# The state product of a chunked linear-attention kernel, head by head into halves of the PSUM partitions

## The chip, the cores and the metric

The kernel runs on one core of a Trainium2 chip. The metric is device time in microseconds (us) from a run of the whole kernel; lower is better. The core has five engines with instruction queues of their own: TensorE (PE in the profile, with its weight loads as PEld), VectorE (DVE), ScalarE (ACT), GpSimd (POOL) and SyncE (SP, which here only issues transfers).

## The reference

Two stages, one after the other. The first is a recurrent attention with decay, for 4 batches x 8 heads x 768 steps, head size 48:

```python
for t in range(S):
    cur = np.einsum('bhd,bhe->bhde', u[None] * kt, vt)
    y[:, :, t] = np.einsum('bhd,bhde->bhe', rt, state + cur)
    state = wt[:, :, :, None] * state + np.einsum('bhd,bhe->bhde', kt, vt)
```

The second adds to each of the 3072 rows (384 wide) a mixture of adapters: 8 experts of rank 16, of which a gate picks two.

```python
logits = x @ w_gate                      # top 2 of 8, softmax over the two
delta[mask] += w[mask, k, None] * ((x[mask] @ A[e]) @ B[e])
return x + delta
```

## The kernel before

The 3072 rows are 24 tiles of 128 steps, six tiles (chunks) for each batch, and a tile holds all 8 heads side by side (8 x 48 = 384). Within a chunk the recurrence is turned into products: sums of the logarithms of the decay (`csA`, `csB`), their exponentials (`expP`, `expN`), decayed r and k (`mult`, line 284, on VectorE into `rk2`), transposes (`tr`, `trev`), scores of each head with a mask (`amm`, line 353, and `aev`, line 359), and y as scores times v (`ymA`, line 397) plus r times the state of the chunk before (`ymS`, line 387). The term with u goes through `rkp` (line 293), `dg` and `dv` (line 322). The second stage then works on the finished y (`xs`) by groups of up to four tiles: transposes (`xk`), gate (`lg`, `g1` to `g4`), and the two adapter products (`z`, `d`).

The state is what the change is about. In `rk2` each head has 64 columns, 48 of data and 16 of zeros, and heads stand in pairs p, with g = 0 or 1 for the first or second of a pair: 4 pairs, 128 columns each. The accumulator `S_acc` is 128 PSUM partitions x 384 f32, seen as (g, p, e). `kv` (line 366) multiplies, for each pair, the 128 columns of k of both heads with the 96 columns of v of both heads, over the 128 steps of the tile, four matmuls in all. Of the result for a pair the blocks k of head 0 with v of head 0 (first 64 partitions, g = 0) and head 1 with head 1 (last 64, g = 1) are wanted; the two crossed blocks are not. `sev` (through the helper's lines 303 on ScalarE or 305 on VectorE) copies the whole accumulator into `S_sb` as bf16, `szero` (line 382) writes zeros over the two crossed blocks, on GpSimd or, with ch = 1, on VectorE, and `ymS` of the next tile uses `S_sb` for both heads of a pair at once. The products with k of several tiles of a batch add up in `S_acc`; it is begun anew at the first chunk of each batch. The last chunk of a batch needs no `kv`, so there are 20 groups of `kv`, `sev` and `szero`.

The order of the work is written out by hand in `PLAN`, a list of words such as `kv:7` (function, tile) or `sev:3.1` (with ch = 1). Every engine carries out its own instructions in the order in which the list issues them, and waits by semaphore for what it reads. Loads of r, k and v from tile 2 on are issued on GpSimd's queue, those of w and the stores on SyncE's.

Two neighbours matter when the matmuls are compared. `amm` takes its operands from 48 partitions that begin at partition 0 or 64, so it uses a part of the rows of the array, while all other matmuls here use 128 rows and 128 columns. `ymA` is eight matmuls of 48 columns, each with weights of its own.

Of the kernel before, what the change touches and what calls it, by code (L numbers as in the profile page):

```python
# [36 lines left out]
aev:3 load_rk:16 xs:1.1 csA:6 trev:4 xk:1 szero:2 expP:6 load_w:8 ba:2.1 amm:4 xs:2.1 mult:5 dv:3 lg:0 szero:3.1
csB:6 tr:5 aev:4 load_w:10 xk:2 expN:6 csA:7 trev:5.1 ymS:3 load_v:16 xkev:1 xkev:2 ymS:4 dg:5 expP:7 ln:8 ymA:3
mult:6 ba:3 dg:4 csB:7 expN:7 load_w:12 rkp:6 amm:5 tr:6 xs:3 xk:3 dgev:5.1 kv:4 lg:2 dv:4 load_w:14 csA:8 trev:6
aev:5 ymA:4 ba:4 sev:4.1 amm:6 expP:8 lg:1 rkp:7 xs:4 szero:4 xkev:3 dv:5.1 csB:8 kv:6 mult:7 lg:3 g1:3 xk:4 expN:8  # L40
ymS:5 csA:9 dg:6 rkp:8 ln:12 xkev:4.1 tr:7 aev:6 load_w:16 expP:9 gexp:3 dg:7 load_B:0 ymA:5 trev:7 z:3 g2:3 ba:5.1
csB:9 dgev:7.1 sev:6 mult:8 expN:9 load_w:18 xs:5.1 amm:7 kv:7 g3:3 lg:4 csA:10 tr:8 ymA:6 sev:7 expP:10 trev:8 kv:8
xk:5 dv:6 aev:7 rkp:9 ba:6 csB:10 g4:3.1 mult:9 tr:9 sev:8 szero:7 kv:9 zw:3 zTm:3 dv:7.1 expN:10 xs:6 zTev:3 csA:11
szero:6 xkev:5 xk:6 trev:9 expP:11 amm:8 ymS:7 xkev:6 mult:10 szero:8 ba:7.1 csB:11 ymA:7 expN:11 dg:9 dg:8 rkp:10
tr:10 aev:8 sev:9.1 xs:7.1 castB:0 csA:12 expP:12 amm:9 ymS:8 dgev:9.1 mult:11 trev:10 xk:7 dv:8 aev:9 rkp:11 csB:12
ymA:8 expN:12 load_w:20 lg:6 tr:11 szero:9 ba:8 d:3.2 xkev:7 trev:11 xs:8 csA:13 lg:7 expP:13 lg:5 oev:3.2 g1:7 d:1
xk:8 csB:13 oev:1 xkev:8.1 expN:13 dv:9 amm:10 d:2 mult:12 ymS:9 csA:14 ba:9 kv:10 dg:10 gexp:7 ymS:10 g2:7 ln:16
ymA:9 aev:10 rkp:13.1 dg:11 dgev:11 tr:12 expP:14 sev:10 oev:2 rkp:12 xs:9 amm:11 dv:10.1 ymA:10 csB:14 aev:11
trev:12.1 expN:14 lg:8 kv:12 mult:13 ba:10.1 rkp:14.1 xs:10.1 g3:7 xk:9 csA:15 d:0.2 szero:10 xk:10 xkev:9 dg:12
expP:15 xkev:10 mult:14 dv:11.1 amm:12 oev:0.2 g4:7 sev:12 szero:12 csB:15 tr:13 expN:15 ymS:11 kv:13 dg:13 ba:11.1  # L50
trev:13 ymA:11 sev:13 csA:16 z:7 xs:11.1 expP:16 tr:14 dgev:13 mult:15 aev:12 zw:7 xk:11 load_w:22 store:0 csB:16
amm:13 lg:10 zTm:7 ymA:12 dv:12 xkev:11.1 ln:20 ba:12 kv:14 lg:11 expN:16 lg:9 trev:14 csA:17 aev:13 dv:13.1 rkp:15
g1:11 ymS:13 zTev:7.1 xs:12 ba:13.1 mult:16 expP:17 sev:14 tr:15 ymA:13 amm:14 xs:13.1 csB:17 gexp:11 xk:12 rkp:16
d:5 szero:13 g2:11 expN:17 xkev:12 xk:13 rkp:18 trev:15 csA:18 trd:16 dg:15 aev:14 expP:18 g3:11 g4:11 dg:14 mult:17
oev:5 z:11 amm:15 csB:18 store:3 dgev:15 kv:15 xkev:13 szero:14 ymS:14 dv:14 rkp:17.1 d:6 expN:18 ymA:14 dv:15 zw:11
csA:19 ba:14 aev:15 sev:15 oev:6 lg:12 ymS:15 szero:15 dg:16 kv:16 lg:13 ymA:15 expP:19 csB:19 ba:15 xs:14 expN:19
amm:16 rkp:19 xk:14 mult:18 zTm:11 sev:16 xs:15 csA:20 kv:18 d:4 xkev:14 aev:16 rkp:21 trd:17 zTev:11.1 xk:15 dg:17
store:1 amm:17 expP:20 ymS:16 oev:4 mult:19 dgev:17 sev:18 ymA:16 csB:20 kv:19 d:8.2 store:2 rkp:22.1 dv:16.1
xkev:15 trd:18 dv:17.1 lg:14 d:11 aev:17 expN:20 ba:16.1 sev:19 csA:21 oev:8.2 mult:20 trd:19 amm:18 xs:16.1 expP:21
lg:15 xk:16 d:9.2 dg:18 csB:21 oev:11 aev:18 szero:16 oev:9.2 ymS:17 rkp:20 ba:17.1 store:5 ymA:17 xkev:16 trd:20  # L60
expN:21 dg:19 kv:20 xs:17.1 amm:19 store:6 csA:22 xk:17 sev:20 szero:19 szero:18 dgev:19 dv:18 mult:21 expP:22 lg:16
# [1 line left out]
xk:18 trd:21 gexp:15 xk:19 sev:21 csA:23 oev:7 dg:20 xkev:18 xkev:19 store:9 expP:23 szero:20 rkp:23 ymS:20 lg:17
aev:20 g2:15 dg:21 lg:18 lg:19 store:7 mult:22 dgev:21 store:11 dv:20.1 amm:21 csB:23 kv:22 z:15 store:10 store:4
ymA:20 ba:20.1 tr:22 g3:15 ymS:21 expN:23 g4:15 aev:21 xs:20.1 ymA:21 zw:15 dv:21 mult:23 ba:21 xk:20 trev:22 zTm:15
xkev:20 amm:22 zTev:15.1 g1:19 tr:23 gexp:19 g2:19 xs:21 sev:22 xk:21 aev:22 d:15 dg:23 store:8 dg:22 d:13.2
# [25 lines left out]
def kernel(  # L92
# [49 lines left out]
    def setD(t, ch):  # L142
        nc.vector.memset(ones, 1.0)
        nc.vector.memset(centre, CENTRE / 128)

    def triangle(o, cmp, base, step):
        nc.gpsimd.affine_select(out=o, in_=ones[:, 0:128], compare_op=cmp, fill=0.0, base=base,
                                pattern=[[step, 128]], channel_multiplier=-step)
# [212 lines left out]
        st[t]["at"] = at  # L361

    def kv(t, ch):
        c = t % NC
        for p in range(P):
            nc.tensor.matmul(S_acc[:, :, p, :],  # L366
                             lhsT=st[t]["rk2"][:, 1, p].rearrange("s a b -> s (a b)"),
                             rhs=st[t]["v16"][:, 2 * p:2 * p + 2, :],
                             start=(c == 0 and p == 0), stop=(p == P - 1), skip_group_check=True)
# [9 lines left out]

    def szero(t, ch):  # L380
        for g in range(2):
            (nc.gpsimd, nc.vector)[ch].memset(st[t]["S"][64 - 64 * g:128 - 64 * g, g], 0.0)  # L382
# [215 lines left out]
```

## Time and profile before

| | us |
|---|---|
| median of 2 runs (85.8 to 85.84) | 85.82 |
| profiled execution, its own time | 85.61 |
| span of its trace | 83.9 |
| TensorE busy | 76.5 (91%), 1214 matmuls |
| VectorE busy | 72.1 (86%), 166 instructions |
| ScalarE busy | 68.3 (81%), 163 instructions |
| GpSimd busy | 57.1 (68%), 113 instructions |

The span runs from the first to the last instruction of the trace; the profiled execution's time is 1.7 us longer than it. A line of a group gives line, engine, operation, what is written and read, shapes and count; then busy time, and mean ns of one. A line of the timeline gives start, duration until the last of the group ends, engine, line and count; a bracket at the end is idle time of the engine just before, and what ended it. Records of matmuls overlap, since each goes in long before the one ahead of it has come out, so start to start is the measure of what one costs.

### The profile page before, as it was taken

What the parts mean: (1) busy time and instruction counts of PE and PEld (TensorE: products, weight loads), DVE (VectorE), ACT (ScalarE), POOL (GpSimd) and SP (SyncE); (2) the same over time, 40 slices, a digit from 0 to 9 for tenths busy, and PEclk for the clock granted to TensorE, in tenths of its full rate; (3) what the DMA queues carried; (4) which work ended last, traced back from release to release, by engine and by line L of the source; (5) the groups of instructions that cost most, each with busy time, mean ns of one, the idle gap of its engine ahead of it and who ended that gap; (6) DMA issues with size and microseconds to landing.
All of it is one profiled execution on the core that took longest, in us unless ns stands there. A gap on an engine that the chain in (4) does not pass through costs nothing.

```text
span 83.9 us, 3133 instructions
## 1 busy us (share of the span) xinstructions
PE 76.5 (91%) x1214; PEld 56.8 (68%) x1214; DVE 72.1 (86%) x166; ACT 68.3 (81%) x163; POOL 57.1 (68%) x113
## 2 busy tenths in 40 slices
PE   3979999999989999999999999999999999998730
PEld 1234568866868879786888887788677898775300
DVE  3007979997999999999999999999999999999650
ACT  1564988999997999899999989979999949878400
POOL 4987925979949798687864697896969581832000
PEclk9999999999999999999999999999999999999995
DMA  0999999999999999999999992997889672272763
GB/s 13 328 388 283 272 289 281 275 272 293 282 211 214 262 254 252 287 293 283 226 212 212 208 225 55 221 295 140 125 200 225 204 289 90 99 281 109 277 250 129
DMA packets 15407, 19.10 MB, mean 228 GB/s; under 512 B 7200, under 2 KB 12320, under 8 KB 15392
## 3 DMA queue, kind: packets, MB, share of 16 engines
q1 hardware_dynamic: 11952, 11.63, 43.5%
q0 software_dynamic: 3152, 6.69, 41.7%
q10 hardware_dynamic: 288, 0.59, 2.1%
q8 instruction: 9, 0.15, 0.7%
q14 instruction: 6, 0.05, 0.2%
HBM read 19.29 MB, written 4.72 MB: 286 GB/s over the span
## 4 chain that ended last, share of the span: by engine, by line
PE 76%; DVE 6%; ACT 6%; DMA 4%; issue 2%; DVEq 1%; ACTq 0%
PE xk_ps L421 10%; PE trp L332 8%; PE a_ps L353 8%; PE y_ps L397 5%; PE cs_ps L254 5%; PE z_ps L497 4%; PE d_ps L534 4%; PE cs_ps L250 4%; PE a_ps L173 4%; DMA w<-in_w_dram 4%; PE s_ps L366 4%; PE y_ps L387 4%; PE cs_ps L245 4%; PE d_ps L533 3%; PE y_ps L403 2%
## 5 line engine op out<-in xcount | busy, mean ns | idle before, releaser
L359 DVE TENSOR_TENSOR at<-a_ps,strict 128x1024 f16<-128x1024 f32 x24 | 29.3, 1220 | 1.2 <-PE a_ps L353 0.8
L322 POOL TENSOR_TENSOR dv<-v,dg 128x384 f16<-128x384 f16 (+1 forms) x24 | 20.4, 859 | 8.6 <-ACT dg L303 4.7
L293 POOL TENSOR_TENSOR rkp<-rk 128x384 f16<-128x384 f16 (+1 forms) x16 | 14.6, 916 | 0.8 <-DMA rk<-in_rk_dram 0.7
L263 ACT ACTIVATE e<-cs_ps 128x384 bf16<-128x384 f32 x24 | 11.9, 494 | 3.3 <-PE cs_ps L254 3.0
L259 ACT ACTIVATE e<-cs_ps 128x384 bf16<-128x384 f32 x24 | 12.1, 503 | 1.6 <-PE cs_ps L250 1.4
L284 DVE TENSOR_TENSOR rk<-rk,e 128x768 bf16<-128x768 f16 x22 | 12.8, 582 | 0.0
L332 PE MATMUL trp<-ident,rk 128*128 128x128 bf16 x144 | 11.1, 219 | 0.4 <-DVE rk L284 0.4
L309 ACT COPY xkT<-xk_ps 128x384 f32<-128x384 f32 (+1 forms) x24 | 10.5, 447 | 0.9 <-PE xk_ps L421 0.6
L382 POOL MEMSET S_sb<- 64x192 bf16 x38 | 9.6, 252 | 2.4 <-DVE S_sb L305 0.5
L332 PEld LDWEIGHTS <-rk 128*128 128x128 bf16 x144 | 9.0, 97 | 2.0 <-DVE rk L284 0.8
L353 PE MATMUL a_ps<-rkT 48*128 48x128 bf16 x192 | 9.5, 219 | 0.1
L309 ACT COPY rkT<-trp 128x512 f32<-128x512 f32 x15 | 9.0, 597 | 0.0
L397 PE MATMUL y_ps<-v,at 128*128 128x48 f16 x192 | 8.7, 183 | 0.0
L250 PE MATMUL cs_ps<-logw,strict 128*128 128x384 f16 x24 | 8.0, 332 | 0.6 <-ACT logw L233 0.6
L303 ACT COPY res<-d_ps 128x384 f32<-128x384 f32 x15 | 7.2, 488 | 1.5 <-PE zT_ps L520 0.9
L353 PEld LDWEIGHTS <-rkT 48*128 48x128 bf16 x192 | 5.5, 94 | 4.1 <-issue 1.8
L293 DVE TENSOR_TENSOR rkp<-rk 128x384 f16<-128x384 f16 (+1 forms) x8 | 3.8, 472 | 5.1 <-DMA rk<-in_rk_dram 5.1
L254 PE MATMUL cs_ps<-logw,ident 128*128 128x384 f16 x24 | 8.0, 335 | 0.2 <-ACT e L259 0.2
L421 PE MATMUL xk_ps<-ident,rkp 128*128 128x128 f16 x72 | 8.0, 220 | 0.0
L421 PE MATMUL xk_ps<-ident,xs 128*128 128x128 f16 x72 | 8.0, 219 | 0.0
L397 PEld LDWEIGHTS <-at 128*128 128x128 f16 x192 | 7.3, 96 | 0.9
L534 PE MATMUL d_ps<-Ball,zT 128*128 128x384 f16 x24 | 7.8, 327 | 0.0
(77 smaller groups left out, 181.2 us busy)
## 6 DMA issues: line engine op xcount, KB each, us to landing
out_dram<-res SPq DMA_DIRECT2D x24, 192.0 KB, 2.1
w_in<-in_w_dram SPq DMA_DIRECT2D x8, 384.0 KB, 13.0
rk<-in_rk_dram POOLq DMA_DIRECT2D x5, 384.0 KB, 14.5
rk<-in_rk_dram POOLq DMA_DIRECT2D x1, 1536.0 KB, 27.7
w<-in_w_dram SPq DMA_DIRECT2D x3, 384.0 KB, 9.1
v<-in_v_dram POOLq DMA_DIRECT2D x3, 384.0 KB, 18.7
rk<-in_rk_dram POOLq DMA_DIRECT2D x1, 768.0 KB, 21.2
v<-in_v_dram POOLq DMA_DIRECT2D x1, 768.0 KB, 29.9
```

What stands on the lines that cost most here:

```text
L254: nc.tensor.matmul(cs_ps[:, 0:HD], lhsT=ident16, rhs=st[t]["logw"], start=False, stop=True, skip_group_check=True)
L259: nc.scalar.activation(out=e2[:, 0], in_=cs_ps[:, 0:HD], func=ACT.Exp)
L263: nc.scalar.activation(out=st[t]["e2"][:, 1], in_=cs_ps[:, 0:HD], func=ACT.Exp, scale=-1.0)
L284: nc.vector.tensor_mul(rk2s[t % 4].rearrange("s m p h d -> s (m p h) d")[:, :, 0:D], st[t]["rk"].rearrange("s m (h d) -> s (m h) d", d=D), ...
L293: (nc.gpsimd, nc.vector)[ch].tensor_mul(x, st[t]["r"], st[t]["k"])
L309: nc.scalar.copy(out=out.bitcast(F32), in_=in_.bitcast(F32))
L322: (nc.gpsimd, nc.gpsimd, nc.vector)[ch].tensor_mul(x, st[t]["v16"], st[t]["dg"].rearrange("p (h o) -> p h o", o=1).to_broadcast([L, H, D]))
L332: nc.tensor.transpose(trp[:, m, p, :], st[t]["rk2"][:, m, p, :, :].rearrange("s a b -> s (a b)"), ident)
L353: nc.tensor.matmul(a_ps[:, g, p, :], lhsT=rkT[base:base + D, 1, p, :], rhs=rkT[base:base + D, 0, p, :], start=True, stop=True)
L359: nc.vector.tensor_mul(at, st[t]["a_ps"].rearrange("s g p f -> s (g p) f"), strict.to_broadcast([128, H, 128]))
L397: nc.tensor.matmul(y_ps[:, h, :], lhsT=st[t]["at"][:, g * P + p, :], rhs=st[t]["v16"][:, h, :], start=(c == 0 and h == 0), stop=(h == H - ...
L421: nc.tensor.transpose(xk_ps[:, 3 * q + j, :], src[:, j * 128:(j + 1) * 128], ident16)
```

## The change

`kv` is written head by head. For each pair there are two matmuls, one for each head: the stationary operand is that head's 64 columns of k, the moving one its 48 columns of v, and the output is the first 64 partitions (g = 0) or the last 64 (g = 1) of `S_acc`. The crossed blocks are never written, and one memset in `setD`, at the start of the kernel, sets the whole accumulator to zero. `szero` and its 20 words in the plan are gone; all other words stand in the same order.

```diff
...
-load_rk:10 expN:2 trev:1 xkev:-2 kv:1 szero:0 xkev:-3 sev:1.1 csA:3 amm:1 mult:2 rkp:2.1 dg:1 dg:0 expP:3 dgev:1
+load_rk:10 expN:2 trev:1 xkev:-2 kv:1 xkev:-3 sev:1.1 csA:3 amm:1 mult:2 rkp:2.1 dg:1 dg:0 expP:3 dgev:1 csB:3
...
     def setD(t, ch):
         nc.vector.memset(ones, 1.0)
         nc.vector.memset(centre, CENTRE / 128)
+        nc.vector.memset(S_acc, 0.0)
...
     def kv(t, ch):
+
         c = t % NC
         for p in range(P):
-            nc.tensor.matmul(S_acc[:, :, p, :],
-                             lhsT=st[t]["rk2"][:, 1, p].rearrange("s a b -> s (a b)"),
-                             rhs=st[t]["v16"][:, 2 * p:2 * p + 2, :],
-                             start=(c == 0 and p == 0), stop=(p == P - 1), skip_group_check=True)
+            for g in range(2):
+                nc.tensor.matmul(S_acc[64 * g:64 * g + 64, g, p, :], lhsT=st[t]["rk2"][:, 1, p, g, :],
+                                 rhs=st[t]["v16"][:, 2 * p + g, :],
+                                 start=(c == 0 and p == 0), stop=(p == P - 1), skip_group_check=True)
...
-    def szero(t, ch):
-        for g in range(2):
-            (nc.gpsimd, nc.vector)[ch].memset(st[t]["S"][64 - 64 * g:128 - 64 * g, g], 0.0)
-
     def ymS(t, ch):
```

More of the change, by code (lines that the diff above doesn't have):

```diff
@@ L32 @@
 load_v:4 mult:1 sev:0.1 load_rk:8 csA:2 xk:-3 warm:5.1 load_w:4 amm:0 expP:2 xk:-2 casts:0 load_v:8 csB:2 aev:0 tr:1
-load_rk:10 expN:2 trev:1 xkev:-2 kv:1 szero:0 xkev:-3 sev:1.1 csA:3 amm:1 mult:2 rkp:2.1 dg:1 dg:0 expP:3 dgev:1
-csB:3 expN:3 aev:1 tr:2 ymA:0 kv:2 xk:-1 dv:0.1 ba:0.1 load_rk:12 ln:4 ymS:1 szero:1 ymA:1 trev:2.1 xkev:-1 csA:4
-dg:2 xs:0.1 amm:2 rkp:3.1 expP:4 mult:3 xk:0 aev:2 load_w:6 load_v:12 csB:4 sev:2 xkev:0 rkp:4.1 expN:4 tr:3 dg:3
-kv:3 csA:5 dv:1.1 trev:3 dgev:3.1 ymS:2 amm:3 expP:5 ymA:2 dv:2.1 ba:1.1 csB:5 mult:4 ln:6 rkp:5 tr:4 sev:3.1 expN:5
@@ L37 @@
[L37 to L61, printed above, removed]
@@ L62 @@
-kv:21 d:10 xkev:17 ymA:18 csB:22 ba:18 ymS:19 dv:19 aev:19 oev:10 ymA:19 d:7 ba:19 amm:20 g1:15 xs:18 expN:22 xs:19
[L63 to L66, printed above, removed]
@@ L72 @@
-store:17 store:21 oev:23.2 d:22.1 store:20 store:23 oev:22.1 store:22
+load_rk:10 expN:2 trev:1 xkev:-2 kv:1 xkev:-3 sev:1.1 csA:3 amm:1 mult:2 rkp:2.1 dg:1 dg:0 expP:3 dgev:1 csB:3
+expN:3 aev:1 tr:2 ymA:0 kv:2 xk:-1 dv:0.1 ba:0.1 load_rk:12 ln:4 ymS:1 ymA:1 trev:2.1 xkev:-1 csA:4 dg:2 xs:0.1
+amm:2 rkp:3.1 expP:4 mult:3 xk:0 aev:2 load_w:6 load_v:12 csB:4 sev:2 xkev:0 rkp:4.1 expN:4 tr:3 dg:3 kv:3 csA:5
+dv:1.1 trev:3 dgev:3.1 ymS:2 amm:3 expP:5 ymA:2 dv:2.1 ba:1.1 csB:5 mult:4 ln:6 rkp:5 tr:4 sev:3.1 expN:5 aev:3
@@ new lines @@
+load_rk:16 xs:1.1 csA:6 trev:4 xk:1 expP:6 load_w:8 ba:2.1 amm:4 xs:2.1 mult:5 dv:3 lg:0 csB:6 tr:5 aev:4 load_w:10
+xk:2 expN:6 csA:7 trev:5.1 ymS:3 load_v:16 xkev:1 xkev:2 ymS:4 dg:5 expP:7 ln:8 ymA:3 mult:6 ba:3 dg:4 csB:7 expN:7
+load_w:12 rkp:6 amm:5 tr:6 xs:3 xk:3 dgev:5.1 kv:4 lg:2 dv:4 load_w:14 csA:8 trev:6 aev:5 ymA:4 ba:4 sev:4.1 amm:6
+expP:8 lg:1 rkp:7 xs:4 xkev:3 dv:5.1 csB:8 kv:6 mult:7 lg:3 g1:3 xk:4 expN:8 ymS:5 csA:9 dg:6 rkp:8 ln:12 xkev:4.1
+tr:7 aev:6 load_w:16 expP:9 gexp:3 dg:7 load_B:0 ymA:5 trev:7 z:3 g2:3 ba:5.1 csB:9 dgev:7.1 sev:6 mult:8 expN:9
@@ new lines @@
+load_w:18 xs:5.1 amm:7 kv:7 g3:3 lg:4 csA:10 tr:8 ymA:6 sev:7 expP:10 trev:8 kv:8 xk:5 dv:6 aev:7 rkp:9 ba:6 csB:10
+g4:3.1 mult:9 tr:9 sev:8 kv:9 zw:3 zTm:3 dv:7.1 expN:10 xs:6 zTev:3 csA:11 xkev:5 xk:6 trev:9 expP:11 amm:8 ymS:7
+xkev:6 mult:10 ba:7.1 csB:11 ymA:7 expN:11 dg:9 dg:8 rkp:10 tr:10 aev:8 sev:9.1 xs:7.1 castB:0 csA:12 expP:12 amm:9
+ymS:8 dgev:9.1 mult:11 trev:10 xk:7 dv:8 aev:9 rkp:11 csB:12 ymA:8 expN:12 load_w:20 lg:6 tr:11 ba:8 d:3.2 xkev:7
+trev:11 xs:8 csA:13 lg:7 expP:13 lg:5 oev:3.2 g1:7 d:1 xk:8 csB:13 oev:1 xkev:8.1 expN:13 dv:9 amm:10 d:2 mult:12
@@ new lines @@
+ymS:9 csA:14 ba:9 kv:10 dg:10 gexp:7 ymS:10 g2:7 ln:16 ymA:9 aev:10 rkp:13.1 dg:11 dgev:11 tr:12 expP:14 sev:10
+oev:2 rkp:12 xs:9 amm:11 dv:10.1 ymA:10 csB:14 aev:11 trev:12.1 expN:14 lg:8 kv:12 mult:13 ba:10.1 rkp:14.1 xs:10.1
+g3:7 xk:9 csA:15 d:0.2 xk:10 xkev:9 dg:12 expP:15 xkev:10 mult:14 dv:11.1 amm:12 oev:0.2 g4:7 sev:12 csB:15 tr:13
+expN:15 ymS:11 kv:13 dg:13 ba:11.1 trev:13 ymA:11 sev:13 csA:16 z:7 xs:11.1 expP:16 tr:14 dgev:13 mult:15 aev:12
+zw:7 xk:11 load_w:22 store:0 csB:16 amm:13 lg:10 zTm:7 ymA:12 dv:12 xkev:11.1 ln:20 ba:12 kv:14 lg:11 expN:16 lg:9
@@ new lines @@
+trev:14 csA:17 aev:13 dv:13.1 rkp:15 g1:11 ymS:13 zTev:7.1 xs:12 ba:13.1 mult:16 expP:17 sev:14 tr:15 ymA:13 amm:14
+xs:13.1 csB:17 gexp:11 xk:12 rkp:16 d:5 g2:11 expN:17 xkev:12 xk:13 rkp:18 trev:15 csA:18 trd:16 dg:15 aev:14
+expP:18 g3:11 g4:11 dg:14 mult:17 oev:5 z:11 amm:15 csB:18 store:3 dgev:15 kv:15 xkev:13 ymS:14 dv:14 rkp:17.1 d:6
+expN:18 ymA:14 dv:15 zw:11 csA:19 ba:14 aev:15 sev:15 oev:6 lg:12 ymS:15 dg:16 kv:16 lg:13 ymA:15 expP:19 csB:19
+ba:15 xs:14 expN:19 amm:16 rkp:19 xk:14 mult:18 zTm:11 sev:16 xs:15 csA:20 kv:18 d:4 xkev:14 aev:16 rkp:21 trd:17
@@ new lines @@
+zTev:11.1 xk:15 dg:17 store:1 amm:17 expP:20 ymS:16 oev:4 mult:19 dgev:17 sev:18 ymA:16 csB:20 kv:19 d:8.2 store:2
+rkp:22.1 dv:16.1 xkev:15 trd:18 dv:17.1 lg:14 d:11 aev:17 expN:20 ba:16.1 sev:19 csA:21 oev:8.2 mult:20 trd:19
+amm:18 xs:16.1 expP:21 lg:15 xk:16 d:9.2 dg:18 csB:21 oev:11 aev:18 oev:9.2 ymS:17 rkp:20 ba:17.1 store:5 ymA:17
+xkev:16 trd:20 expN:21 dg:19 kv:20 xs:17.1 amm:19 store:6 csA:22 xk:17 sev:20 dgev:19 dv:18 mult:21 expP:22 lg:16
+kv:21 d:10 xkev:17 ymA:18 csB:22 ba:18 ymS:19 dv:19 aev:19 oev:10 ymA:19 d:7 ba:19 amm:20 g1:15 xs:18 expN:22 xs:19
@@ new lines @@
+xk:18 trd:21 gexp:15 xk:19 sev:21 csA:23 oev:7 dg:20 xkev:18 xkev:19 store:9 expP:23 rkp:23 ymS:20 lg:17 aev:20
+g2:15 dg:21 lg:18 lg:19 store:7 mult:22 dgev:21 store:11 dv:20.1 amm:21 csB:23 kv:22 z:15 store:10 store:4 ymA:20
+ba:20.1 tr:22 g3:15 ymS:21 expN:23 g4:15 aev:21 xs:20.1 ymA:21 zw:15 dv:21 mult:23 ba:21 xk:20 trev:22 zTm:15
+xkev:20 amm:22 zTev:15.1 g1:19 tr:23 gexp:19 g2:19 xs:21 sev:22 xk:21 aev:22 d:15 dg:23 store:8 dg:22 d:13.2 g3:19
+xkev:21 oev:15 z:19 d:14 trev:23 g4:19 oev:13.2 amm:23 zw:19 dgev:23 oev:14 dv:22.1 store:15 d:12 aev:23 store:13
@@ new lines @@
+store:14 ymS:22 dv:23 ymA:22 ba:22.1 lg:20 oev:12 lg:21 xs:22.1 g1:21 zTm:19 ymS:23 ba:23 ymA:23 xs:23 zTev:19.1
+xk:22 d:18.2 clr:23 xkev:22 gexp:21 oev:18.2 lg:22 xk:23 store:12 d:19 xkev:23 d:16 oev:19 g1:22 g2:21 g3:21 lg:23
+oev:16 z:21 gexp:22 g1:23 d:17 gexp:23 g4:21 zw:21 zTm:21 g2:22 oev:17 z:22 zTev:21.1 z:23 g2:23 zw:22 d:21.2 zw:23
+d:20 store:18 oev:20 zTm:23 oev:21.2 zTm:22 zTev:22 store:19 zTev:23.1 store:16 d:23.2 store:17 store:21 oev:23.2
+d:22.1 store:20 store:23 oev:22.1 store:22
```

5 lines of the change are left out of this document (removed).

## The prediction

> **What bounds the kernel now.** I read the page first: the busy shares, the slices, and the engines of the chain that ended last.
>
> ```profile
> span 83.9 us, 3133 instructions
> PE 76.5 (91%) x1214; PEld 56.8 (68%) x1214; DVE 72.1 (86%) x166; ACT 68.3 (81%) x163; POOL 57.1 (68%) x113
> PE   3979999999989999999999999999999999998730
> PE 76%; DVE 6%; ACT 6%; DMA 4%; issue 2%; DVEq 1%; ACTq 0%
> ```
>
> TensorE (PE) carries 76% of the chain and shows a 9 in almost every slice from the third on; GpSimd (POOL) has room, at 68%. A busy PE need not be a full PE, so the next view is the busy time by stretch (window, then busy time and count for each engine):
>
> ```profile
> 0.00:10.00 10.00, 8.00 (x36) 3.54 (x37) 3.86 (x8) 5.17 (x9) 8.05 (x21) 1.00 0.83 256
> 10.00:20.00 10.00, 9.55 (x153) 7.15 (x151) 9.46 (x17) 9.11 (x23) 6.57 (x12) 1.00 1.08 281
> 20.00:75.00 55.00, 54.47 (x991) 43.79 (x990) 53.65 (x123) 50.87 (x122) 42.06 (x80) 1.00 0.91 217
> 75.00:83.90 8.90, 4.46 (x39) 2.29 (x39) 5.13 (x21) 3.15 (x11) 0.43 (x2) 0.89 0.54 202
> ```
>
> From 20 to 75 us PE stands idle 55.00 - 54.47 = 0.53 us in all. VectorE (DVE) is almost as full there (53.65), yet it gives the chain only 6%: what PE has to do sets the pace, and a nanosecond added to PE in this stretch is nearly a nanosecond of the span. Before 20 us it is less so (0.45 us idle between 10 and 20), and the tail from 75 us on holds neither the state product nor the zeroing.
>
> Busy time of a matmul says little, as each record is about 0.2 us long while the next starts long before. What a matmul costs is the step from its start to the next start. The timeline of PE gives it:
>
> ```profile
> 53.88 0.33 PE L534 MATMUL d_ps<-Ball,zT 128*128 128x384 f16 x1
> 54.05 0.36 PE L397 MATMUL y_ps<-v,at 128*128 128x48 f16 x8
> 54.25 0.32 PE L245 MATMUL cs_ps<-logw,co 128*128 128x384 f16 x1
> 54.41 0.32 PE L250 MATMUL cs_ps<-logw,strict 128*128 128x384 f16 x1
> ...
> 54.65 0.33 PE L387 MATMUL y_ps<-S_sb,rkT 128*128 128x96 bf16 x4
> 54.82 0.22 PE L298 MATMUL s_ps<-w,xkT 128*128 128x8 f16 x3
> 54.90 0.33 PE L366 MATMUL s_ps<-v,rk 128*128 128x96 f16 x4
> 55.06 0.22 PE L436 MATMUL s_ps<-w,xkT 128*128 128x8 f16 x3
> 55.14 0.36 PE L397 MATMUL y_ps<-v,at 128*128 128x48 f16 x8
> 55.34 0.32 PE L254 MATMUL cs_ps<-logw,ident 128*128 128x384 f16 x1
> 55.60 0.40 PE L353 MATMUL a_ps<-rkT 48*128 48x128 bf16 x8
> 55.93 0.34 PE L421 MATMUL xk_ps<-ident,rkp 128*128 128x128 f16 x3
> 56.11 0.33 PE L421 MATMUL xk_ps<-ident,xs 128*128 128x128 f16 x3
> ```
>
> Four readings carry the sum. The state product of today (L366, four matmuls of 96 columns) takes from 54.90 to 55.06, and the like group L387 from 54.65 to 54.82: 0.17 us. Eight matmuls of 48 columns with eight different weights (L397) take 0.20 us (54.05 to 54.25, 55.14 to 55.34): 25 ns each, so at 48 columns it is not the columns that count. A single matmul of 384 columns takes 0.16 us to the next start (54.25 to 54.41), but 0.26 us when the next is L353 (55.34 to 55.60): going in to L353 costs 0.10 us. And L353 ends at 56.00; its last matmul, 217 ns long, so starts at 55.78, and the next line starts 0.15 us later at 55.93, where a step of 128 columns is 0.18 / 3 = 0.06 us (55.93 to 56.11): coming out costs 0.09 us. The three steps between its four pairs take 0.18 us, 0.06 us a pair: the two matmuls of a pair run side by side.
>
> ```profile
> L353 PE MATMUL a_ps<-rkT x192: 213/217/228, 10.6 to 72.9; 48*128 48x128 bf16 x192
> ```
>
> What sets L353 apart is that its matmuls use a part of the array: 48 rows from partition 0 or 64, and not all 128. The loads of the weights say the same thing from the other side:
>
> ```profile
> 55.12 0.27 PEld L397 LDWEIGHTS <-at 128*128 128x128 f16 x8
> 55.32 0.10 PEld L254 LDWEIGHTS <-ident 128*128 128x128 f16 x1
> 55.59 0.23 PEld L353 LDWEIGHTS <-rkT 48*128 48x128 bf16 x8 [0.18 <-issue]
> 55.92 0.17 PEld L421 LDWEIGHTS <-rkp 128*128 128x128 f16 x3
> ```
>
> L254's weights are there 20 ns ahead of its matmul while L397 still runs; L353's come only 10 ns ahead, after 0.18 us in which the loader waited for nothing that the profile shows. So the array seems to be emptied first.
>
> **The change part by part.**
>
> *Zeroing gone.* 38 memsets on GpSimd leave, 38 x 252 ns = 9.6 us, and two on VectorE, 2 x 138 ns = 0.28 us:
>
> ```profile
> L382 POOL MEMSET S_sb<- x38: 251/252/253, 10.7 to 72.1; 64x192 bf16 x38
> L382 DVE MEMSET S_sb<- x2: 138/138/138, 20.3 to 20.5; 64x96 uint32 x2
>   POOL dv L322: 1.1, 1
>   POOL gs L476: 0.3, 1
> ```
>
> The last two lines are from the list of who waited for these memsets: only GpSimd's own next instructions, 1.4 us together. No line of PE waits for GpSimd in the whole list of waits. So I cost their removal at nothing; the cover is PE's full queue. All that stood behind them on GpSimd (rkp, dv, gs, g, and four loads issued on its queue) starts up to 0.5 us earlier for each pair passed. VectorE's 0.28 us lies at 20.3 us, ahead of a stretch in which PE sets the chain; worth 0 to 0.28, taken as 0. One side effect has a size: the product rk ran 1282 ns once, where others take some 550 ns, beside a GpSimd product that started with it.
>
> ```profile
> 22.73 1.28 DVE L284 TENSOR_TENSOR rk<-rk,e 128x768 bf16<-128x768 f16 x1
> 22.66 0.92 POOL L293 TENSOR_TENSOR rkp<-rk 128x384 f16<-128x384 f16 x1
> 29.30 0.55 DVE L284 TENSOR_TENSOR rk<-rk,e 128x768 bf16<-128x768 f16 x1
> ```
>
> With GpSimd moved, this meeting can vanish or another arise: -0.7 to +0.7 us, taken as 0.
>
> *One memset of the state's accumulator at the start* (VectorE, 128x384 f32 in PSUM). Not in the trace; the nearest rows are the eviction of that same area and the memsets beside it:
>
> ```profile
> L305 DVE CAST S_sb<-s_ps x5: 543/547/552, 10.1 to 35.2; 128x384 bf16<-128x384 f32 x5
> 1.37 0.38 DVE L144 MEMSET centre<- 128x384 f16 x1
> 6.89 1.28 DVE L293 TENSOR_TENSOR rkp<-rk 128x384 f16<-128x384 f32 x1 [5.14 <-DMA rk<-in_rk_dram]
> ```
>
> It takes 0.38 to 0.55 us, behind the last memset and inside the 5.14 us in which VectorE waits for the first rk. No cost; without that cover it would be its half microsecond.
>
> *The state product.* Twenty groups of four matmuls become twenty groups of eight: each head's 64 stationary columns, 48 moving columns, output in 64 of the PSUM partitions. Moving work per output column is the same in sum, but each matmul now uses half of the array's columns, a form that is nowhere in the trace. Its cost is made from the two nearest rows: eight matmuls of 48 columns at L397's 25 ns, 0.20 us, and L353's going in and coming out, 0.10 + 0.09 = 0.19 us, since it too uses a part of the array. That is 0.39 us against 0.17 us now, +0.22 us a group.
>
> The bounds. From below: no cost of going in and out, and pairs side by side as in L353, 4 x 25 = 0.10 us, which is -0.07 us a group. From above: the weights of each head, no longer a whole set of 128 columns, are not hidden behind the matmul before. A load's record is 97 ns for 128 columns:
>
> ```profile
> L366 PEld LDWEIGHTS <-rk x80: 95/97/99, 9.5 to 67.4; 128*128 128x128 bf16 x80
> ```
>
> Half of it, 48 ns for 64 columns, is an estimate from that row; 8 x 48 + 190 = 0.57 us, +0.41 us a group. I take +0.22, because L397 matches in columns and number of weights and L353 is the only row with part of the array.
>
> [...]
>
> *The sum.* How the groups lie (window, then PE's busy time and matmuls of L366):
>
> ```profile
> 0.00:20.00 20.00, 1.34 (x16) 0.88 (x16) 1.00 0.95 269
> 20.00:75.00 55.00, 5.32 (x64) 3.82 (x64) 1.00 0.91 217
> ```
>
> Sixteen groups stand in the full stretch: 16 x 0.22 = 3.52 us. Four stand before 20 us, where PE has gaps: half counts, 0.44 us. In the plan the groups of tiles 7 and 20 stand next to an L353 group, so one going out and one going in become one: -0.19 us for the two. Of the 0.53 us idle in the stretch, half may be filled: -0.26 us. Sum +3.5 us. The evictions of the state (ACT and DVE) and the y products behind them come later by as much as PE does, and lose the 0.5 us of zeroing between them, so no new wait follows. The profiled execution's own time is 85.61 us, hence 89.1 us; the median of the runs shown is 0.21 us above it, hence **89.3 us**.
>
> **The rivals.**
>
> *The pairs run side by side.* The two halves of a pair use different columns, as L353's use different rows, and L353 does take 0.06 us a pair. Then 4 x 25 + 190 = 0.29 us, +0.12 us a group: 16 x 0.12 + 0.24 - 0.19 - 0.26 = +1.7 us, 87.5 us. For it stands L353; against it that 25 ns may be the loading of one set of weights, which side by side does not shorten. [...]
>
> *Weights not hidden.* +0.41 us a group: 16 x 0.41 + 0.82 - 0.19 - 0.26 = +6.9 us, 92.7 us. For it: a load of half a set is a form that the trace lacks. Against it: every load in the trace is hidden but those at L353's start.
>
> *No emptying for columns, matmuls one by one.* 0.20 against 0.17 us, +0.03 us a group: +0.3 us, 86.1 us, no change.
>
> *The other side: neither emptying nor one by one.* 0.10 against 0.17 us, -0.07 us a group, 20 x -0.07 = -1.4 us at most, 84.4 us. It decides at a group of 0.17 us: below that the kernel is not slower. It needs both that columns differ from rows in the emptying and that they are like them in running side by side, which is why I give it little. GpSimd's freed 9.6 us adds nothing to it while PE stays full.
>
> **How the numbers follow.** Forecast (one by one, with emptying) 0.42, weights not hidden in part or whole 0.20, side by side with emptying 0.18, no emptying 0.14, the other side 0.06. The likeliest gives 89.3 us; alone it would range from 88.4 to 90.3, by the 0.7 us of the GpSimd meeting and the shares of gaps filled. The range, 86.1 to 92.7 us, reaches from no emptying to weights not hidden. Two per cent of 85.82 is 1.7 us, about what a measurement can tell from no change, so the borders are 84.1 and 87.5. Side by side ends on that border and is halved. The other side is halved too: half stays near its 84.4, half falls below 84.1 if the GpSimd meeting vanishes as well. Slower: 0.42 + 0.20 + 0.09 = 0.71; the same: 0.09 + 0.14 + 0.03 = 0.26; faster: 0.03.
>
> **What would show it.** In the timeline of the changed kernel, the step from the first start of a state product to the next line's start is 0.30 us (eight at 25 ns and the way out), and the line before it is followed 0.10 us late, with a gap of the loader marked as issue ahead of the group. A step between the matmuls near 3 ns and then 25 would be the pairs; near 50 ns or more, the weights. PE would still show no wait for GpSimd, and GpSimd's busy time would be near 47.5 us. It is wrong if the groups cost no more than 0.2 us all told, or if PE begins to wait for VectorE or ScalarE, so that the added time is lost in gaps or grows beyond the sum.

## The result, and the profile after

| | before | after |
|---|---|---|
| median of two runs each, us | 85.82 | 89.48 (89.22 to 89.74) |
| ratio of the runs, 95% interval | 1 | 1.0456, 1.0386 to 1.0525 |
| profiled execution, its own time, us | 85.61 | 89.22 |
| span of its trace, us | 83.9 | 87.5 |

The change makes the kernel 4.6% slower. The forecast was 89.3 us, so the time came out almost as foretold. The experiments show that two terms of the sum were off and made up for each other: the way in and out of each group was sized rightly, the closeness of the total is luck. Medians are of all runs of a kernel, ratios of its fast runs alone: some executions of one and the same kernel are over 1.5% longer and are left out of the ratios.

First the page after: span, busy shares, GpSimd's slices, and the engines of the chain that ended last.

```profile
span 87.5 us, 3237 instructions
PE 79.8 (91%) x1294; PEld 57.6 (66%) x1294; DVE 74.2 (85%) x165; ACT 69.3 (79%) x163; POOL 48.5 (55%) x75
POOL 4989406769779494094721876882809161352000
PE 69%; DVE 11%; DMA 7%; ACT 6%; issue 2%; DVEq 1%; ACTq 0%
```

GpSimd (POOL) is busy for 8.6 us less, though memsets of 9.6 us are gone, because three of its products rkp now take 1.23 to 1.24 us in place of 0.91. TensorE (PE) gained 80 matmuls, as the change says. But PE carries 69% of the chain where it carried 76%, and VectorE (DVE) 11% where it carried 6%: not all of the added time is PE's. PE idles more too. In the full stretch, which now ends at 78.6 us, the stretch view has

```profile
20.00:78.60 58.60, 57.39 (x1057) 44.62 (x1056) 55.84 (x122) 52.38 (x124) 34.96 (x47) 1.00 0.89 204
```

1.21 us without a matmul, against 0.53 before. The timeline of PE shows what a state product (now L368) costs, and that of the weight loads beside it shows why:

```profile
26.43 0.32 PE L254 MATMUL cs_ps<-logw,ident 128*128 128x384 f16 x1
26.69 0.31 PE L368 MATMUL s_ps<-v,rk 128*64 128x48 f16 x8
26.93 0.23 PE L433 MATMUL s_ps<-w,xkT 128*128 128x8 f16 x3
```

```profile
26.38 0.10 PEld L254 LDWEIGHTS <-ident 128*128 128x128 f16 x1
26.69 0.20 PEld L368 LDWEIGHTS <-rk 128*64 128x64 bf16 x8 [0.21 <-issue]
26.92 0.14 PEld L433 LDWEIGHTS <-xkT 128*128 128x128 f16 x3
```

L254 is followed after 0.26 us, where 0.16 is its step alone: 0.10 us to go in, and the loader stands idle 0.21 us for nothing that the profile shows, as ahead of the scores. The eight matmuls end at 27.00; one lasts 189 ns, so the last starts at 26.81, seven steps took 0.12 us (17 ns each in the mean), and the next line comes 0.12 us later: about 0.10 us to come out. A group costs 0.10 + 0.24 = 0.34 us here against 0.17, and 0.31 where a short matmul stands ahead of it (0.07 to go in): +0.14 to +0.17 us.

The mean of 17 ns hides that the matmuls go in twos. By their start times in the trace the seven steps are 3, 49, 4, 28, 3, 29 and 3 ns: the two of a pair begin 3 or 4 ns apart, and after the first, slower pair the next pair follows 32 ns after the one before. The timeline cut off at 26.71 us, 0.02 us after the first start, has two of the eight already:

```profile
26.69 0.21 PE L368 MATMUL s_ps<-v,rk 128*64 128x48 f16 x2
```

The rest goes with VectorE's rk products. First their group in the kernel before and in the changed one, then the timeline of all engines around one of them:

```profile
L284 DVE TENSOR_TENSOR rk<-rk,e 128x768 bf16<-128x768 f16 x22 | 12.8, 582 | 0.0
L284 DVE TENSOR_TENSOR rk<-rk,e 128x768 bf16<-128x768 f16 x22 | 14.2, 647 | 0.0
```

```profile
31.84 0.83 POOL L322 TENSOR_TENSOR dv<-v,dg 128x384 f16<-128x384 f16 x1
31.85 1.23 DVE L284 TENSOR_TENSOR rk<-rk,e 128x768 bf16<-128x768 f16 x1
...
33.14 0.34 PE L332 MATMUL trp<-ident,rk 128*128 128x128 bf16 x3 [0.35 <-DVE rk L284]
```

The mean of the rk products is 647 ns; it was 582. Five of them take over 700 ns, where one did. This one takes 1.23 us: GpSimd's product dv stands where the two memsets stood before and begins 0.01 us ahead of it. The transposes on PE then wait for it. But a wait of this kind is in the kernel before too, behind its one slow product. What is new on PE are three waits of 0.2 us each (first the wait for rk before, then the three new ones after). The first of the three is for `sel`, which VectorE computes some 0.4 us behind the slow rk product at 26.64 us:

```profile
24.07 0.62 PE L332 MATMUL trp<-ident,rk 128*128 128x128 bf16 x8 [0.38 <-DVE rk L284]
```

```profile
28.23 0.22 PE L298 MATMUL s_ps<-w,xkT 128*128 128x8 f16 x3 [0.23 <-DVE sel L451]
67.90 0.40 PE L353 MATMUL a_ps<-rkT 48*128 48x128 bf16 x8 [0.21 <-DMA rkT<-rk]
68.98 0.33 PE L418 MATMUL xk_ps<-ident,rkp 128*128 128x128 f16 x3 [0.24 <-ACT res L303]
```

### The profile page after: what moved, and what is told of

It is laid out like the page before. It is cut to its first block, busy times and chain, and to the rows that moved or that the text cites. A ratio compares the mean times of both kernels' runs of the same rounds, so it can differ in the third digit from the quotient of the medians.

```text
span 87.5 us, 3237 instructions
## 1 busy us (share of the span) xinstructions
PE 79.8 (91%) x1294; PEld 57.6 (66%) x1294; DVE 74.2 (85%) x165; ACT 69.3 (79%) x163; POOL 48.5 (55%) x75
## 4 chain that ended last, share of the span: by engine, by line
PE 69%; DVE 11%; DMA 7%; ACT 6%; issue 2%; DVEq 1%; ACTq 0%
PE xk_ps L418 8%; PE trp L332 7%; PE a_ps L353 7%; PE cs_ps L254 5%; PE y_ps L394 4%; PE a_ps L173 4%; PE d_ps L531 4%; PE cs_ps L250 4%; DMA out_dram<-res 4%; PE y_ps L384 4%; PE s_ps L368 4%; PE z_ps L494 4%; DMA w<-in_w_dram 3%; PE cs_ps L245 3%; DVE at L359 3%; DVE rk L284 3%
## 5 line engine op out<-in xcount | busy, mean ns | idle before, releaser
L359 DVE TENSOR_TENSOR at<-a_ps,strict 128x1024 f16<-128x1024 f32 x24 | 29.2, 1218 | 2.7 <-PE a_ps L353 2.6
L293 POOL TENSOR_TENSOR rkp<-rk 128x384 f16<-128x384 f16 (+1 forms) x16 | 15.5, 977 | 0.3 <-DMA rk<-in_rk_dram 0.3
L263 ACT ACTIVATE e<-cs_ps 128x384 bf16<-128x384 f32 x24 | 11.8, 492 | 3.5 <-PE cs_ps L254 3.1
L284 DVE TENSOR_TENSOR rk<-rk,e 128x768 bf16<-128x768 f16 x22 | 14.2, 647 | 0.0
L254 PE MATMUL cs_ps<-logw,ident 128*128 128x384 f16 x24 | 8.0, 334 | 0.2 <-ACT e L259 0.2
L173 PE MATMUL a_ps<-ones 128*128 128x512 f16 x17 | 6.9, 526 | 1.4 <-DVE ones L142 1.4
L303 ACT CAST S_sb<-s_ps 128x384 bf16<-128x384 f32 x15 | 7.2, 482 | 0.4 <-DVE dg L305 0.3
```

The source lines that it names most:

```text
L254: nc.tensor.matmul(cs_ps[:, 0:HD], lhsT=ident16, rhs=st[t]["logw"], start=False, stop=True, skip_group_check=True)
L284: nc.vector.tensor_mul(rk2s[t % 4].rearrange("s m p h d -> s (m p h) d")[:, :, 0:D], st[t]["rk"].rearrange("s m (h d) -> s (m h) d", d=D), ...
L293: (nc.gpsimd, nc.vector)[ch].tensor_mul(x, st[t]["r"], st[t]["k"])
L303: nc.scalar.copy(out=out, in_=in_)
L359: nc.vector.tensor_mul(at, st[t]["a_ps"].rearrange("s g p f -> s (g p) f"), strict.to_broadcast([128, H, 128]))
```

## The experiments

Times are medians, with the ratio to the kernel before run beside it. The kernel before itself spread from 85.0 to 86.9 us in one of these jobs, in part by when the first loads land (the first masking of scores, L359, starts between 10.6 and 11.8 us). So beside each time stands the stretch of the trace from that first masking to the end, which is the span less the first start in L359's row: before 83.9 - 11.1 = 72.8 us, after 87.5 - 11.5 = 76.0 us.

```profile
L359 DVE TENSOR_TENSOR at<-a_ps,strict x24: 1209/1220/1225, 11.1 to 73.2; 128x1024 f16<-128x1024 f32 x24
```

```profile
L359 DVE TENSOR_TENSOR at<-a_ps,strict x24: 1206/1217/1225, 11.5 to 76.8; 128x1024 f16<-128x1024 f32 x24
```

| run | us | ratio, 95% interval | stretch, us | of the 22 rk products of 128x768, over 700 ns |
|---|---|---|---|---|
| before | 85.82 | | 72.8 | 1 |
| after | 89.48 | 1.0456, 1.0386 to 1.0525 | 76.0 | 5 |
| after_again | 89.07 | 1.0383, 1.0329 to 1.0436 | 76.4 | 5 |
| kv8_full | 86.82 | 1.0126, 1.0036 to 1.0216 | 73.8 | 1 |
| kv_split | 91.73 | 1.0756, 1.0658 to 1.0853 | 78.8 | 4 |
| kv_unpaired | 88.64 | 1.0270, 1.0218 to 1.0322 | 76.2 | 4 |
| kv_by_amm | 89.89 | 1.0409, 1.0343 to 1.0475 | 77.3 | 5 |
| after_zero_kept | 88.85 | 1.0377, 1.0289 to 1.0465 | 75.4 | 1 |
| before_no_zero | 87.02 | 1.0169, 1.0090 to 1.0249 | 74.5 | 5 |
| before_scratch_zero | 85.25 | 0.9888, 0.9829 to 0.9947 | 72.7 | 1 |
| before_delay6 | 85.75 | 0.9995, 0.9952 to 1.0039 | 73.0 | 1 |
| before_delay6b | 86.48 | 1.0058, 1.0016 to 1.0100 | 74.3 | 1 |
| before_delay6c | 85.16 | 0.9979, 0.9942 to 1.0017 | 72.5 | 0 |
| diag_copies | 89.03 | 1.0384, 1.0326 to 1.0442 | 76.2 | 6 |

Each stretch is that of one execution, and the two of the changed kernel differ by 0.4 us. In after_zero_kept and diag_copies one early rk product of 128x384 is slow as well, before the stretch begins.

My theory after the result: the groups cost some 2.9 us of the span through going in and coming out, and the rest comes from GpSimd's products, which now begin beside VectorE's rk products. The rivals were the count of matmuls and loads, and TensorE alone.

**kv8_full: eight matmuls, but of the whole array**

```diff
             for g in range(2):
-                nc.tensor.matmul(S_acc[64 * g:64 * g + 64, g, p, :], lhsT=st[t]["rk2"][:, 1, p, g, :],
+                nc.tensor.matmul(S_acc[:, g, p, :], lhsT=st[t]["rk2"][:, 1, p].rearrange("s a b -> s (a b)"),
```

> The kernel before, with its zeroing, but the state product as eight matmuls of 48 columns that each use all 128 stationary columns: the count of matmuls of the change without its use of half of the columns. Theory (what the change costs is going in to and coming out of a part of the array): a group takes 8 x 25 = 0.20 us against 0.17, no emptying around it, so 86.0 to 86.6 us. Rival (the count of matmuls and weight loads costs it): most of the 3.7 us are here too, 88.5 us or more.

It took 86.82 us, 1.3% over the kernel before and a little over what was expected. The stretch rose by 1.0 us, against 3.2 in the changed kernel. PE's timeline:

```profile
26.67 0.32 PE L254 MATMUL cs_ps<-logw,ident 128*128 128x384 f16 x1
26.83 0.36 PE L367 MATMUL s_ps<-v,rk 128*128 128x48 f16 x8
27.03 0.22 PE L436 MATMUL s_ps<-w,xkT 128*128 128x8 f16 x3
```

L254 keeps its 0.16 us, the eight take 0.20, and nothing is paid on either side. So the count costs 0.03 us a group, some 0.6 us in all, and what the changed kernel pays to go in and come out, 0.10 us each, goes with the use of half of the columns. The rest of the 1.0 us is idle time of PE: 56.30 - 55.35 = 0.95 us between 20 and 76.3 us, against 0.53 before.

**kv_split: two ways in and out in place of one**

```diff
-        for p in range(P):
+        for p in range(2 * ch, 2 * ch + 2):
...
-kv:4 lg:2
+kv:4 lg:2 kv:4.1
```

> The changed kernel with each state product cut into two halves of four matmuls (pairs 0 and 1, pairs 2 and 3), with the next line of TensorE's order between them; in 17 of the 20 groups that line uses the whole array, once it is the scores, twice nothing lies between. No matmul is added. Theory (emptying): 17 more ways in and out at 0.19 us and one at 0.09, and the 0.02 us by which a first pair is slower than the others, so +2.8 to +3.5 us over the changed kernel, 92.2 to 93.0 us. Rival (count and weights): no more than 0.5 us over it, 89.2 to 90.0 us.

91.73 us: 2.3 us over the first measurement of the changed kernel and 2.7 over the second, and in the stretch +2.8 or +2.4 us. This is less than expected but far from the rival's 0.5. The timeline shows the second payment:

```profile
26.67 0.32 PE L254 MATMUL cs_ps<-logw,ident 128*128 128x384 f16 x1
26.93 0.24 PE L367 MATMUL s_ps<-v,rk 128*64 128x48 f16 x4
27.10 0.23 PE L432 MATMUL s_ps<-w,xkT 128*128 128x8 f16 x3
27.26 0.24 PE L367 MATMUL s_ps<-v,rk 128*64 128x48 f16 x4
27.44 0.34 PE L417 MATMUL xk_ps<-ident,rkp 128*128 128x128 f16 x3
```

Half a group takes 0.17 us to the next line where the whole one took 0.24, and the gate's three short matmuls in between (L432), which take 0.08 us elsewhere (26.59 to 26.67 in kv8_full), take 0.16. Doubling the suspected cost raised the time without a matmul more.

**kv_unpaired: the halves one after the other**

```diff
-        for p in range(P):
-            for g in range(2):
+        for g in range(2):
+            for p in range(P):
```

> The changed kernel with the loops of the state product turned round: first the four matmuls into the first 64 partitions, then the four into the last 64, so that neighbours no longer use different columns. Theory (two matmuls side by side take 0.03 us together because they use different columns): most steps are 0.03 us for one matmul and not for two, a group takes 0.08 to 0.1 us more, 90.5 to 91.5 us. Rival (the step is a matter of issue, whatever the columns): 89.2 to 89.8 us, as the changed kernel.

The theory fell: the stretch is 76.2 us, between the two of the changed kernel (76.0 and 76.4), and the group takes 0.26 us where it took 0.24:

```profile
25.90 0.32 PE L368 MATMUL s_ps<-v,rk 128*64 128x48 f16 x8
26.16 0.23 PE L433 MATMUL s_ps<-w,xkT 128*128 128x8 f16 x3
```

For the group it makes next to no difference whether neighbours use different columns. The single steps do change, to 14, 39, 13, 19, 13, 18 and 14 ns, so the steps of 3 ns go with the order in which the halves alternate, but two matmuls together still take 32 ns. A matmul with 64 stationary columns so follows the one ahead after 17 to 19 ns in the mean in either order, where one with 128 takes 25. What sets the 32 ns is not settled. The median is 0.8 us below the first of the changed kernel, but the first masking starts 0.8 us earlier too (10.7 us), and that is the loads.

**kv_by_amm: next to the scores**

```diff
-rkp:6 amm:5 tr:6 xs:3 xk:3 dgev:5.1 kv:4 lg:2
+rkp:6 amm:5 kv:4 tr:6 xs:3 xk:3 dgev:5.1 lg:2
```

These lines show one of the 12 moves.

> The changed kernel with 12 more of the state products moved, by two to four places in TensorE's order, to stand next to a group of scores (14 of 20 then do). Theory (one emptying does for leaving the part of the rows and entering the part of the columns): 12 ways in at 0.09 us less, 88.1 to 88.9 us, if no eviction comes too late by the move. Rival (each of the two has a way in and out of its own): 89.2 to 89.8 us.

Neither came true: 89.89 us is just above the rival's range, and the stretch is 0.9 or 1.3 us longer than the two of the changed kernel, in an execution (90.57 us) that is the slowest of its four. The saving itself exists and stands already in the changed kernel's timeline, where tile 7 follows the scores:

```profile
30.12 0.40 PE L353 MATMUL a_ps<-rkT 48*128 48x128 bf16 x8
30.45 0.31 PE L368 MATMUL s_ps<-v,rk 128*64 128x48 f16 x8
30.69 0.23 PE L433 MATMUL s_ps<-w,xkT 128*128 128x8 f16 x3
```

The scores take 0.33 us to the next line, as ahead of any other, and nothing is paid to go in. In the other order, too, a product moved ahead of the scores mostly pays nothing to come out, 0.24 us to the next line:

```profile
58.84 0.31 PE L367 MATMUL s_ps<-v,rk 128*64 128x48 f16 x8
59.08 0.40 PE L352 MATMUL a_ps<-rkT 48*128 48x128 bf16 x8
```

Four of the five groups ahead of scores in this trace take 0.24 us and one takes 0.30. But the moved products put later work off: PE is idle 60.00 - 58.06 = 1.94 us between 20 and 80 us,

```profile
20.00:80.00 60.00, 58.06 (x1065) 45.53 (x1064) 57.06 (x122) 52.61 (x126) 35.53 (x47) 1.00 0.88 199
```

against 1.21 us in the changed kernel. Which of the moves does it was not tried.

**before_no_zero, before_scratch_zero and after_zero_kept: GpSimd's part by itself**

The first takes the zeroing out of the kernel before, the second writes it into a scratch tile in the same places, the third puts it back into the changed kernel.

```diff
     def szero(t, ch):
         for g in range(2):
-            (nc.gpsimd, nc.vector)[ch].memset(st[t]["S"][64 - 64 * g:128 - 64 * g, g], 0.0)
+            (nc.gpsimd, nc.vector)[ch].memset(scr[64 - 64 * g:128 - 64 * g, g], 0.0)
```

> The kernel before with its zeroing left out and nothing else (the crossed blocks of the state then add terms that the reference has not): the freeing of GpSimd alone. Theory (no engine that sets the pace waits for the zeroing): within 0.7 us of 85.8, up or down, by how many of VectorE's rk products meet one of GpSimd's products. Rival (the 9.6 us of GpSimd are on the way of the state to the y product): 84.1 us or less.

> The kernel before with its 40 memsets in their places but into a scratch tile that nobody reads (the crossed blocks of the state add terms that the reference has not). Theory (the memsets cost nothing, and what made their removal slower is that GpSimd's products then started beside VectorE's rk products): the time of the kernel before, 85.3 to 86.2 us, and at most two rk products over 700 ns. Rival (it is slower without the zeroing for another reason, such as the lost wait): 86.6 to 87.4 us.

> The changed kernel with the 40 memsets of the crossed blocks kept where they stood in the kernel before, writing zeros over zeros: the state product of the change with GpSimd's old timing. Theory (the groups cost 0.33 against 0.17 us, some 2.9 us of the span, and the rest is that GpSimd, freed, meets VectorE's rk products more often): 88.4 to 89.0 us, with two slow rk products at most where the changed kernel has five. Rival (GpSimd's timing is of no account and TensorE alone makes the difference): 89.2 to 89.8 us.

Taking 9.6 us of work off GpSimd, and 0.28 off VectorE, makes the kernel slower: 87.02 us, 1.7% (0.9 to 2.5), 1.7 us in the stretch. That is outside the 0.7 us of the theory, and the other way from the rival. The same memsets into a tile that nobody reads bring the old stretch back (72.7 us, 85.25 us). So their place in the queue is what counts. Two things in the trace of before_no_zero, its slowest execution of four (87.37 us), go with the 1.7 us. Five rk products are slow, and the mean of the group is 652 ns; and, by the list of waits, PE once waits 1.1 us for a transpose by DMA of rk:

```profile
L283 DVE TENSOR_TENSOR rk<-rk,e 128x768 bf16<-128x768 f16 x22 | 14.4, 652 | 0.0
```

```profile
PE a_ps L352 <- DMA rkT<-rk: 1.1, 1, 1.1
```

The rk of that transpose took 0.89 us, 0.34 more than most. But the transpose itself also took longer than any of the kernel before. Of the six from issue to landing (min/median/max, us), first before, then before_no_zero:

```profile
DMA to landing us min/median/max: 3.0/3.1/3.3
DMA to landing us min/median/max: 3.1/3.2/4.8
```

Transposes of 4.6 to 4.8 us are also in kv8_full, after_zero_kept and before_delay6b, which have their memsets and one slow rk product of 128x768 each. So how much of GpSimd's part comes through the slow rk products, and how much through these transposes, is not settled; that it comes with the place of the memsets is shown.

In the changed kernel, keeping the memsets gives 88.85 us and a stretch of 75.4 us, where without them it is 76.0 and, in after_again, 76.4. The same spot as above in its timeline:

```profile
32.41 0.55 DVE L285 TENSOR_TENSOR rk<-rk,e 128x768 bf16<-128x768 f16 x1
32.50 0.56 POOL L384 MEMSET S_sb<- 64x192 bf16 x2
...
33.03 0.82 POOL L323 TENSOR_TENSOR dv<-v,dg 128x384 f16<-128x384 f16 x1
```

rk lies beside the memsets, takes 0.55 us, and dv begins when it is done. The intervals of the two medians overlap (1.0289 to 1.0465 and 1.0386 to 1.0525), so it is the traces alone, one of the kernel with the memsets and two without, that carry the 0.6 to 1.0 us. PE's idle time is less by about as much, 0.71 us here against 1.21, in a window that again ends 8.9 us before the end:

```profile
20.00:78.30 58.30, 57.59 (x1063) 44.96 (x1060) 55.26 (x124) 52.84 (x125) 43.45 (x81) 1.00 0.89 205
```

**before_delay6, 6b and 6c: the one slow rk product of the kernel before**

```diff
+    def fill(t, ch):
+        nc.gpsimd.memset(scr, 0.0)
...
-rkp:6
+fill:6 rkp:6
```

The scratch tile is 128x64 here and 128x640 in 6b; 6c writes it in two halves of 64x192.

> The kernel before with one small memset of a scratch tile on GpSimd ahead of the product rkp of tile 6, so that this product starts some 0.15 us later than the rk product that it held up, and not 0.07 us earlier. Theory (of two such products the one that starts first holds up the other): the rk product takes 0.55 us in place of 1.28, and the kernel 84.9 to 85.4 us. Rival (they slow each other whichever is first, or the time is lost again behind): 85.6 us or more.

> As before_delay6 but with a memset ten times as long, some 0.6 to 0.8 us, since the short one moved the product rkp of tile 6 by only a few hundredths. Theory (the rk product is held up until a GpSimd product that has the operands first is done): no rk product over 700 ns, and 0.3 to 0.7 us less than the kernel before. Rival (they slow each other in any order, or the time is lost again behind): no difference from the kernel before.

> As before_delay6b, but the delay ahead of the product rkp of tile 6 is made of two memsets of 64x192, in the form of the zeroing, some 0.56 us together, where one long memset made the rk product slower still (1.86 us), though it began 0.5 us ahead of rkp. Theory (a GpSimd product takes hold of the operands when the instruction ahead of it begins, so the order that counts is rk against the second memset): rk is ahead of the second memset, takes 0.55 us, no rk product is over 700 ns, and the trace from the first masking to the end is 72.2 to 72.5 us against 72.8. Rival (rk waits for the end of whatever product is next on GpSimd): it takes 1.7 us or more again, and that stretch is 73 us or more.

The first moved rkp too little: it began 0.03 us after rk, and rk took 1.38 us. In 6b rk began 0.52 us ahead of rkp and was slower still, which goes against the theory that the start of rkp counts. The timeline:

```profile
22.26 0.65 POOL L386 MEMSET scr<- 128x640 bf16 x1
22.34 1.86 DVE L285 TENSOR_TENSOR rk<-rk,e 128x768 bf16<-128x768 f16 x1
22.86 0.93 POOL L294 TENSOR_TENSOR rkp<-rk 128x384 f16<-128x384 f16 x1
```

rk and rkp end together but for 0.4 us (24.20 and 23.79). The stretch of 6b, 74.3 us, also holds a wait of PE of 0.7 us for a transpose by DMA. In 6c two memsets make a delay of about the same length, and rk passes:

```profile
22.87 0.56 POOL L387 MEMSET scr<- 64x192 bf16 x2
22.91 0.55 DVE L285 TENSOR_TENSOR rk<-rk,e 128x768 bf16<-128x768 f16 x1
...
23.40 0.91 POOL L294 TENSOR_TENSOR rkp<-rk 128x384 f16<-128x384 f16 x1
```

rk takes 0.55 us though a memset began 0.04 us ahead of it, and no rk product is over 700 ns. The stretch, 72.5 us, is within what was expected, and the rival (rk waits for whatever product is next) is out. This fits the theory that GpSimd's product counts from the start of the instruction ahead of it: in 6b that was 0.08 us before rk, in 6c it is the second memset, which begins after rk. The memsets differ in partitions too (128 and 64), so this is the reading that fits, not proof, and no run shows what would hold rk up. With 0.9979 (0.9942 to 1.0017) the time cannot be told from the kernel before's.

**after_again and diag_copies**

```diff
-        x = wk.tile([128, 2, P, D], BF16, name="S_sb", bufs=3)
-        copy(ch, x, S_acc)
+        x = S_sbs[sum(i % NC < NC - 1 for i in range(t)) % 3]
+        for g in range(2):
+            copy(ch, x[64 * g:64 * g + 64, g], S_acc[64 * g:64 * g + 64, g])
```

The three tiles of S_sbs are set to zero once, at the start.

> The changed kernel once more, since its first measurement rests on two runs: 88.6 to 89.7 us, and in the trace 75.8 to 76.2 us from the first masking of scores to the end, with four or five slow rk products.

> No zeroing and no half products: the state product of the kernel before, three state tiles zeroed once at the start, and the eviction as two copies that take only the wanted blocks (64 partitions x 192 each). TensorE's groups stay at 0.17 us; each eviction costs ScalarE or VectorE one more instruction, some 0.2 to 0.3 us each. Theory (freeing GpSimd moves its products beside the rk products, as without the zeroing): four or five slow rk products and 86.8 to 88.0 us. Rival (with no cost on TensorE the missing zeroing is a gain): 85.5 us or less.

The repeat gave 89.07 us, within what was expected, and the same five slow products; its stretch of 76.4 us is 0.2 over. Doing without the zeroing by copying only the wanted blocks took 89.03 us, a miss above the 88.0 expected, with six slow rk products. Its row of evictions shows 312 ns for half the columns and half the partitions, so two cost 0.62 us where one took 0.48:

```profile
L305 ACT CAST S_sb<-s_ps 64x192 bf16<-64x192 f32 x30 | 9.4, 312 | 0.6 <-DVE dg L307 0.2
```

How its 3.3 us divide between evictions and slow products was not taken apart.

## Why the prediction was right, point by point

- **What bounds the kernel: right.** PE's order and fullness set the pace. Changes of a tenth of a microsecond a group show in the time (kv_split). The sentence that no new wait follows was wrong: PE's idle time in the full stretch rose from 0.53 to 1.21 us, and two of the three new waits are for VectorE and ScalarE.
- **Going in and coming out, 0.10 + 0.09 us taken from the scores' rows: right.** Measured 0.10 (0.07 behind a short matmul) and 0.10.
- **Eight matmuls one by one at 25 ns, 0.20 us: wrong.** The matmuls go in twos, 32 ns for two after a slower first pair, and seven steps took 0.12 us. The group came to 0.31 to 0.34 us and not 0.39, so +0.14 to +0.17 a group in place of +0.22. The steps are those that the prediction named as the sign of its rival "side by side", near 3 ns and then some 25. The rival foretold 0.29 us, and the group lies between, because a pair takes 32 ns and not 25 and the first one some 20 ns more. The rival's reason, different columns, explains the 3 ns but not the 32: by kv_unpaired two matmuls in the same columns take as long.
- **The sum over the groups.** With +0.17 in the same formula: 16 x 0.17 + 4 x 0.085 - 0.19 - 0.26 = +2.6 us. after_zero_kept against before, the groups without GpSimd's part, has 75.4 - 72.8 = +2.6 us. In part this is chance. By the start times in those two traces, the nineteen groups of the stretch, with what it costs to go in and come out, take 3.6 us before and 6.1 in after_zero_kept, +2.5 us, and nearly all of it shows in the time, as the prediction said of PE. But no idle time was filled: between 20 us and 8.9 us before the end PE is idle for 0.71 us, where it was 0.53, so the term of -0.26 did not come about. It made up for groups that cost less than +0.17 in the mean.
- **The two groups next to the scores: right for one, half right for the other.** Scores and then state product save the whole way in. The changed kernel's one state product ahead of scores is followed by them after 0.29 us where the usual is 0.24 (64.45 and 64.74 in the lines below), so half of the 0.10 is still paid. It is not a rule of this order, since four of the five such groups in kv_by_amm pay nothing; why this one does was not found.

```profile
64.45 0.31 PE L368 MATMUL s_ps<-v,rk 128*64 128x48 f16 x8
64.74 0.40 PE L353 MATMUL a_ps<-rkT 48*128 48x128 bf16 x8
```

- **Zeroing gone, at nothing: wrong in its size, with the right place named.** No engine that sets the pace waited for the memsets, but they kept GpSimd's products apart from VectorE's rk. The prediction put this meeting at -0.7 to +0.7 us and took 0. It is +0.6 us in the changed kernel (76.0 - 75.4; +1.0 by after_again) and +1.7 us alone. The two do not add, since 2.6 + 1.7 is more than the 3.2 measured; that a PE with longer groups hides part of it is a guess that no run tests. GpSimd's busy time is 48.5 us and not near 47.5, by the three products that were held up.
- **Why the total fitted.** In the stretch 2.6 + 0.6 = 3.2 us, two differences of the same three traces, which must add up. The first group and the time of the first loads add 0.4 ahead of it, and the span grows by 3.6. The forecast had 3.5 from the groups alone. Too much for the matmuls and too little for GpSimd balanced by luck; with the right step alone it would have said 88.4.
- **The memset at the start: right.** 378 ns, with VectorE idle for 4.22 us behind it:

```profile
1.82 0.38 DVE L144 MEMSET s_ps<- 128x384 f32 x1
6.41 1.27 DVE L293 TENSOR_TENSOR rkp<-rk 128x384 f16<-128x384 f32 x1 [4.22 <-DMA rk<-in_rk_dram]
```

## What to carry to other kernels

Half the columns was not half the price here: a group took 0.31 to 0.34 us against 0.17, some 0.2 us of it for going in and coming out, so such a product could pay only where a group saves more than that, or where it stands next to the scores and shares their way in or out (behind them a group took 0.24 us and nothing to go in). No run here shows one that pays. Work on an engine with room may still be useful where it stands, as a spacer (the kernel before without its memsets was 1.7 us longer in the stretch); before removing it, look at which products on GpSimd and VectorE will then begin together (rk took 1.23 us beside dv and 0.55 beside the memsets), and at which transfers will start at another time. And where runs spread by a microsecond, measure inside the trace, from a landmark behind the first loads to the end.
